# Cosine layer of an attention, experts and cosine kernel: three blocks of token tiles in place of four

## The chip, the cores and the metric

One core of a Trainium2 chip runs the whole kernel in one launch. The metric is the device time of the launch in microseconds (us). TensorE does the matmuls, ScalarE (ACT) and VectorE (DVE) the elementwise work, GpSimd (POOL) some of it and the gathers, SyncE (SP) issues most DMAs. Results of TensorE go to eight banks of 128 x 512 float32.

## The reference

Attention with pooled queries gives x with 1152 rows of 512. A layer of eight experts with the top two per row (`w1`, ReLU, `w2`) gives a new x. Then the cosine layer, which the change is about:

```python
def _moe2_ref(x, w_in, w_out) -> np.ndarray:   # x 1152 x 512, w_in 512 x 2048, w_out 2048 x 512
    h = x @ w_in
    g = h * np.cos(h)
    return (g @ w_out).astype(np.float32)
```

## The kernel before

The 1152 rows are nine tiles of 128. Every float32 operand is kept as a high and a low part, and each product is made of three matmuls (`mm3`, L1043: high x high, high x low, low x high; the matmul itself is L1048).

**The cosine layer** (from L1143, loop at L1454) takes the tiles in blocks, `BLK`: (0, 1), (2, 3), (4, 5) and (6, 7, 8). For each block it runs over f = 0 to 15, the sixteen groups of 128 hidden columns; a step is one (block, f), and the loop runs through the 64 steps in one go.

- `g_mm(b, f)` (L1346): h of all rows of the block in one result bank, twelve matmuls (four groups of inputs x three), each 128 columns wide per tile of the block.
- `g_head` (L1387), `g_cos` (L1403), `g_split` (L1412): cosine by range reduction and the two parts of g = h cos h. The nine instructions go ScalarE L1398 (or L1377), VectorE L1399 to L1401 (or L1378 to L1380), ScalarE Abs and Sin (L1408, L1409 or L1383, L1384), VectorE product (L1410 or L1385), ScalarE `gh` (L1416), VectorE `gl` (L1417). In a block of 256 columns the intermediate r lies in the second half of the same bank, so `gl`, the last instruction, still reads it; in wider blocks it lies in `cr`, and the product is the bank's last reader.
- `o_mm(b, f)` (L1420): for each tile of the block three matmuls of 512 columns, added up over f in one bank per tile (`OA`).

In one turn of the loop, the order is: combine (below), `g_mm` of step i, `o_mm` of step i - 3 (`LAG`, L1453), `g_cos` of step i - 1, `g_head` of step i, `g_split` of step i - 1, then, in the first block only, the split of one more unit of cosine weights into its parts (`conv`, L622: ScalarE L624, then POOL or, at step 6, VectorE L625). Each engine works through its instructions in this order.

**Combining the next block.** While block b runs, the tiles of block b + 1 are made from the outputs of the experts: `comb_load` (L1148, at f in `CL`, and f = 9 for a third tile) gathers two rows per token with two DMAs issued by POOL; `comb` (L1155, at f in `CM`) scales the first on ScalarE into a result bank `CS` (L1166) and adds the second on VectorE (L1167); `comb_tr` (L1180, at f in `CT`) transposes with four short TensorE instructions (L1173) into a `t` bank and copies out with ScalarE (L1185) and VectorE (L1186).

**Result banks.** Of the eight, two have the name `t` (`tb2`, L1001), and at L1335 three are given to `h` (`h_bank`, L1004) and so three to `acc` (`a_bank`, L1007, for `OA`, `CS` and the last expert's third piece). Tiles of one name take its banks in turn, and a new tile waits until the last reader of the old one in that bank is done. `g_mm` of overall step s takes `t` if s mod 3 is 2, else `h`; `comb_t` and `small_weights` (L518) take `t` too.

**The end of a block.** `o_out` (L1443) copies each `OA` with ScalarE to a buffer `os` (three of them) and stores it from SP; the last block goes through `o_last` (L1429), which shares the copies between ScalarE and VectorE, halves the last one and stores from ScalarE's queue. The weights were loaded through a ring of three buffers `raw` (`raw_load`, L607), not used after the first block.

Of the kernel before, what the change touches and what calls it, by code (L numbers as in the profile page):

```python
# [9 lines left out]
F32 = mybir.dt.float32  # L10
F32R = mybir.dt.float32r
# [3 lines left out]
AF = mybir.ActivationFunctionType  # L15
OP = mybir.AluOpType
AX = mybir.AxisListType
PSUM = bass.MemoryType.PSUM
# [4 lines left out]
def attn_moe_cos_kernel(ctx, tc, q, k, v, w_gate, w_noise, noise, w1, w2, w_in, w_out, out):  # L23
    nc = tc.nc
# [3 lines left out]
    DM = H * D  # L28
# [489 lines left out]
    def small_weights(k):  # L518
        m = CNT8[:, 1:2]
        if k:  # L520
            p = tb2()
            nc.tensor.matmul(p[:, 0:2], ONES, FLB, start=True, stop=True)
            nc.vector.tensor_scalar(m, p[:, 0:1], TOP, TOP, op0=OP.mult, op1=OP.min)
            nc.vector.tensor_tensor(CNT, CNT8[:, 0:1], m, op=OP.max)
            return
        nc.vector.tensor_reduce(m, FL, axis=AX.X, op=OP.max)
        nc.vector.tensor_scalar(FLB, m.to_broadcast([128, 2]), 0.0, None, op0=OP.is_gt)
# [68 lines left out]
    NU, NA, RB, NX = 12, 3, 3, 4  # L596
    U, UX, RAW, rawp = [], [], {}, []
# [51 lines left out]
    def advance_c(c):  # L649
        advance(min(c + RB, len(SEQ)), c)  # L650
# [106 lines left out]
    t = t0 = Q2[0, 0] = qk.tile([128, 1216], F32R, name="q2", bufs=3)  # L757
# [16 lines left out]
    c = slice(0, SQ)  # L774
# [30 lines left out]
    c = slice(SQ, 1216)  # L805
# [39 lines left out]
    for n in range(NTOT - 1):  # L845
        hp, hl, t = tiles[n]
# [57 lines left out]
    n = NTOT - 1  # L904
# [92 lines left out]
    mes = ExitStack()  # L997
    mpe = ExitStack()
    mp = [mpe.enter_context(tc.tile_pool(name="moeps", bufs=1, space=PSUM, reuse_waits="tile")), 2]
# [21 lines left out]
    me = mx.enter_context(tc.tile_pool(name="moee", bufs=1, reuse_waits="tile"))  # L1021
# [84 lines left out]

    def y_out(e, st):
        o = ACC.pop((e, st))
        t = mb.tile([128, DM], F32, name="os", bufs=3) if st == 2 else me.tile([128, DM], F32, name="ys", bufs=3)
        n = SW[e][st][1]  # L1110
        if st == 1:
            nc.vector.tensor_copy(t[128 - n:128], o[128 - n:128])
        else:
            nc.scalar.activation(t[128 - n:128], o[128 - n:128], AF.Copy)
        y_store(nc.scalar, e, st, n, t[128 - n:128])
# [24 lines left out]

    DEC, DW = {}, {}

    BLK = [(0, 1), (2, 3), (4, 5), (6, 7, 8)]  # L1143
    G2, CB, CS, X2, LM, hb, hes = {}, {}, {}, {}, {}, [], ExitStack()
    WS = const.tile([128, 2], F32, name="WS")
    RF = const.tile([128, 2, 2, 2], F32, name="RF")
# [1 line left out]
    def comb_load(t):  # L1148
        for j in range(2):
            g = G2[t, j] = hb[0].tile([128, DM], F32, name="g", bufs=4)  # L1150
            nc.gpsimd.indirect_dma_start(
                out=g, out_offset=None, in_=y_d[0:min(t + 1, 3) * 1024],
                in_offset=bass.IndirectOffsetOnAxis(ap=ROWC[:, t, j:j + 1], axis=0))

    def comb(b, i):  # L1155
        t = BLK[b][i]
        g0, g1 = G2.pop((t, 0)), G2.pop((t, 1))
# [16 lines left out]
        return p.rearrange("p (a s) -> p a s", a=4), slice(128 * i, 128 * i + 128)  # L1174

    def x2_tile(b):
        pool, w = (mb, 384) if b % 2 else (hb[0], 256)
        X2[b] = tuple(pool.tile([128, 4, w], F32R, name=f"x2{k}") for k in range(2))

    def comb_tr(b, i):  # L1180
# [55 lines left out]
        nc.scalar.activation(LM["x"][:, :, cs], pv, AF.Copy)  # L1236

    def x2_parts():
        xp_, (xh, xl) = LM["x"], X2[0]
        for h in range(2):  # L1240
            p = tb2()
            ks = slice(2 * h, 2 * h + 2)
            for k in range(2):
                seq = [(y[:, st, 256 * h + 128 * k:256 * h + 128 * k + 128], LM["o"][:, st])
                       for y in LM["y"] for st in range(2)]
                for i, (l, r) in enumerate(seq):
                    nc.tensor.matmul(p[:, 256 * k:256 * k + 256], l, r, start=(i == 0), stop=(i == 3))
            x = xp_[:, ks]
            nc.vector.tensor_tensor(x, p.rearrange("p (a s) -> p a s", a=2), x, op=OP.add)
            nc.scalar.activation(xh[:, ks], x, AF.Copy)  # L1250
            nc.vector.tensor_tensor(xl[:, ks], x, xh.bitcast(F32)[:, ks], op=OP.subtract)

    LA = 6
    YS = (4, 7, 1)
    CL = (2, 6)
    CM = (6, 9, 11)
    CT = (8, 12, 13)
    CO = 4
    LOD = (6,)
    LMS = (18, 25, 26, 27, 28, 34)  # L1260
    NF2 = FF2 // 128
# [14 lines left out]
    for e in range(E_N):  # L1276
        last = e == E_N - 1
        for f in range(8):
            s = 8 * e + f
# [52 lines left out]
    for st in range(2):  # L1332
        y_out(E_N - 1, st)
    mpe.close()
    mp[:] = [mes.enter_context(tc.tile_pool(name="mm2ps", bufs=1, space=PSUM, reuse_waits="tile")), 3]  # L1335
    HS = {(0, 0): h_bank()}
    for f in range(YS[0]):
        y_mm(E_N - 1, f, 2)
# [6 lines left out]
        y_mm(E_N - 1, f, 2)  # L1345
    def g_mm(b, f):  # L1346
        nb = len(BLK[b]) * 128
        p = HS.pop((b, f)) if (b, f) in HS else (tb2 if (NF2 * b + f) % 3 == 2 else h_bank)()
        o = p[:, 0:nb]
        w = unit(NCONV + f)[:, :, 0:512].rearrange("p s (a f) -> p s a f", a=4)  # L1350
        xh, xl = X2[b]
        mm3(o, [(w[:, 0, kd], w[:, 1, kd], xh[:, kd, 0:nb], xl[:, kd, 0:nb]) for kd in range(4)], True, True)
        HS[b, f] = p
# [10 lines left out]
    mb = m2.enter_context(tc.tile_pool(name="m2", bufs=1, reuse_waits="tile"))  # L1364
# [9 lines left out]
    GT, OA = {}, {}  # L1374
# [12 lines left out]
    def g_head(b, f):  # L1387
        nb = len(BLK[b]) * 128
        p = HS[b, f]
        o = p[:, 0:nb]  # L1390
        n, c = (mb.tile([128, 384], F32, name=nm, bufs=2)[:, 0:nb] for nm in ("cn", "cr"))
        if 2 * nb > 512:
            HS[b, f] = (o, c, c)
            cos_arg(n, c, o)
            return
        r = p[:, nb:2 * nb]
        HS[b, f] = (o, r, c)
        nc.scalar.activation(r, o, AF.Identity, scale=1.0 / (2.0 * math.pi), bias=MGC[:, 0:1])  # L1398
        nc.vector.tensor_scalar(n, r, MAGIC, None, op0=OP.subtract)  # L1399
        nc.vector.scalar_tensor_tensor(r, n, -C1, o, op0=OP.mult, op1=OP.add)  # L1400
        nc.vector.scalar_tensor_tensor(r, n, -C2, r, op0=OP.mult, op1=OP.add)  # L1401
# [10 lines left out]
    def g_split(b, f):  # L1412
        nb = len(BLK[b]) * 128
        o, r, c = HS.pop((b, f))
        gh, gl = (mb.tile([128, 384], F32R, name=nm, bufs=4) for nm in ("gh", "gl"))
        nc.scalar.activation(gh[:, 0:nb], r, AF.Copy)  # L1416
        nc.vector.tensor_tensor(gl[:, 0:nb], r, gh.bitcast(F32)[:, 0:nb], op=OP.subtract)  # L1417
        GT[b, f] = (gh, gl)

    def o_mm(b, f):  # L1420
        gh, gl = GT.pop((b, f))
        w = unit(NCONV + f)[:, :, 512:1024]
        for i in range(len(BLK[b])):
            if f == 0:
# [1 line left out]
            c = slice(128 * i, 128 * i + 128)  # L1426
            mm3(OA[b, i], [(gh[:, c], gl[:, c], w[:, 0], w[:, 1])], f == 0, f == NF2 - 1)

    def o_last(b):  # L1429
        n = len(BLK[b])  # L1430
        for i, t in enumerate(BLK[b]):
            s = mb.tile([128, DM], F32, name="os", bufs=3)
            o = OA.pop((b, i))
            if i == n - 1:
                nc.scalar.activation(s[:, 0:256], o[:, 0:256], AF.Copy)
                nc.vector.tensor_copy(s[:, 256:512], o[:, 256:512])
            elif i % 2:
                nc.vector.tensor_copy(s, o)
            else:
                nc.scalar.activation(s, o, AF.Copy)  # L1440
            nc.scalar.dma_start(out[t * 128:(t + 1) * 128], s)

    def o_out(b):  # L1443
        if b == len(BLK) - 1:
            o_last(b)
            return
        for i, t in enumerate(BLK[b]):
            s = mb.tile([128, DM], F32, name="os", bufs=3)
            nc.scalar.activation(s, OA.pop((b, i)), AF.Copy)
            nc.sync.dma_start(out[t * 128:(t + 1) * 128], s)  # L1450

    steps = [(b, f) for b in range(len(BLK)) for f in range(NF2)]
    LAG = 3  # L1453
    for i in range(len(steps) + LAG):  # L1454
        if i < len(steps):
            b, f = steps[i]
            if b + 1 < len(BLK):
                nx = BLK[b + 1]
                for q_, t in enumerate(nx[:2]):
                    if f == CL[q_]:  # L1460
                        comb_load(t)
                if f == 9 and len(nx) > 2:
                    comb_load(nx[2])
                for q_, t in enumerate(nx):
                    if f == CM[q_]:
                        comb(b + 1, q_)
                    if f == CT[q_]:
                        comb_tr(b + 1, q_)
            if i > 1:
                g_mm(b, f)  # L1470
        if i >= LAG:
            b, f = steps[i - LAG]
            o_mm(b, f)
            if f == NF2 - 1:
                o_out(b)
        if 0 < i <= len(steps):
            g_cos(*steps[i - 1])
        if i < len(steps):
            g_head(*steps[i])
        if i == YS[2]:  # L1480
            y_out(E_N - 1, 2)
        if i in (3 * NF2 + 2, 3 * NF2 + 7):
            small_weights(i != 3 * NF2 + 2)
        if 0 < i <= len(steps):
            g_split(*steps[i - 1])
        if i < NF2:
            st_w["lo"] = nc.vector if i in LOD else nc.gpsimd
            advance_c(min(NCONV + i + CO, len(SEQ)))
# [121 lines left out]
```

## Time and profile before

| | |
|---|---|
| time, median of 3 runs (lowest to highest) | 772.87 us (767.8 to 774.36) |
| the profiled execution: its own time, its span | 777.81 us, 776.2 us |
| cosine layer within the span | from about 560 us to 770 us |
| first block, steps g0 to g15 | g0 from 560.2, g15 at 602.7 us |
| last block, steps 48 to 63 | from 698 us |

The profile gives, for one execution, each instruction's start and duration, the idle time of its engine just before it and what released it ("<-DVE gl L1417": VectorE's instruction at line 1417 writing `gl`). "x12" is twelve merged instructions. PE is TensorE. Matmuls overlap at their ends, so the time per matmul is read from the chain of waits, not from the mean of one.

### The profile page before, as it was taken

Reading aid. Unit: us, or ns where it says so; the run is one execution under the profiler, and the core shown is the slowest. Engines: PE = TensorE matmul, PEld = TensorE weight load, DVE = VectorE, ACT = ScalarE, POOL = GpSimd, SP = SyncE. Lnnn points to the kernel's source line nnn. Section 1 sums busy time; section 2 is a strip of 40 time slices with the busy share of each in tenths; the row PEclk is TensorE's granted clock in tenths of the full one; section 3 lists DMA queues with packets and bytes.
Section 4 is the critical chain, followed back from the end, with each engine's and each line's share of the span. In section 5 each row is a group of like instructions: output and inputs, shape, how many; then the busy total and the mean of one; then the engine's idle time right before and its main releaser. Section 6 shows DMA issues by size and latency. Waiting matters only on the chain.

```text
span 776.2 us, 14241 instructions
## 1 busy us (share of the span) xinstructions
PE 742.8 (96%) x4977; PEld 690.5 (89%) x4977; DVE 573.4 (74%) x1235; ACT 529.6 (68%) x1256; POOL 287.1 (37%) x338
## 2 busy tenths in 40 slices
PE   7899999999999987799999999999999999999996
PEld 4699999999999987699899999998889999999895
DVE  5778788778888885368888886776668687785663
ACT  5898799879979842248667766756478665765542
POOL 5978867867868758200000000002067010000000
PEclk9999999999999999799999999999999999999998
DMA  9847757676488716678989989877444110100001
GB/s 219 176 112 186 173 135 170 148 192 147 107 208 295 230 31 235 220 227 298 343 300 328 339 294 324 295 267 244 160 112 141 55 55 2 55 0 28 2 1 43
DMA packets 80125, 133.86 MB, mean 172 GB/s; under 512 B 12394, under 2 KB 42474, under 8 KB 80046
## 3 DMA queue, kind: packets, MB, share of 16 engines
q1 hardware_dynamic: 73230, 110.67, 49.1%
q0 software_dynamic: 5376, 18.40, 6.5%
q10 hardware_dynamic: 1440, 3.80, 1.8%
q8 instruction: 41, 0.67, 0.4%
q14 instruction: 38, 0.31, 0.1%
HBM read 80.99 MB, written 30.29 MB: 143 GB/s over the span
## 4 chain that ended last, share of the span: by engine, by line
PE 82%; DMA 5%; ACT 4%; DVE 3%; issue 3%; POOL 1%; SPq 1%; ACTq 0%; DVEq 0%; POOLq 0%
PE h L1048 22%; PE acc L1048 13%; PE acc L1080 12%; PE s L297 10%; PE pa L369 8%; PE pt L331 8%; PE t L1048 4%; PE t L1040 1%; DMA qd<-ql 1%; DMA raw<-w_d 1%; DMA kb<-sh 1%; PE pt L674 1%; PE t L1097 1%; DMA kt<-st 1%; ACT u L624 1%
## 5 line engine op out<-in xcount | busy, mean ns | idle before, releaser
L316 ACT ACTIVATE p<-s,nm 128x384 f32<-128x384 f32 x216 | 126.1, 593 | 1.2 <-DVE nm L309 0.8
L307 DVE TENSOR_REDUCE nm<-s 128x1 f32<-128x384 f32 x216 | 108.4, 549 | 25.1 <-PE s L297 24.4
L1048 PE MATMUL h<-xe,u 128*128 128x320 f32 (+5 forms) x768 | 122.4, 309 | 2.0 <-issue 2.0
L1048 PEld LDWEIGHTS h<-xe,u 128*128 128x128 f32 x768 | 110.8, 190 | 5.5 <-issue 3.7
L625 DVE TENSOR_TENSOR u<-raw,u 128x1024 fp32r<-128x1024 f32 x66 | 80.5, 1223 | 32.4 <-ACT u L624 32.3
L331 PE MATMUL pt<-ident,p 128*128 128x128 f32 x645 | 93.5, 272 | 0.5 <-ACT st L179 0.3
L297 PE MATMUL s<-kt,q 128*128 128x384 f32 x240 | 84.7, 368 | 4.6 <-DMA kt<-st 2.2
L369 PE MATMUL pa<-eh,v 128*128 128x320 f32 (+1 forms) x279 | 86.5, 324 | 0.0
L344 ACT ACTIVATE eh<-pt 128x384 fp32r<-128x384 f32 x144 | 63.0, 491 | 31.5 <-PE pt L331 29.4
L1135 POOL DMA_DIRECT2D w_d<-dw x16 | 8.5, 534 | 202.7 <-DVE dw L1134 202.7
L369 PE MATMUL pa<-el,v 128*128 128x320 f32 (+1 forms) x279 | 82.3, 309 | 0.0
L624 ACT ACTIVATE u<-raw 128x1024 fp32r<-128x1024 f32 x73 | 76.7, 1055 | 7.0 <-DMA raw<-w_d 3.0
L331 PEld LDWEIGHTS pt<-ident,p 128*128 128x128 f32 x645 | 77.6, 140 | 3.8 <-ACT st L179 0.6
L1080 PE MATMUL acc<-hh,u 128*128 128x320 f32 (+5 forms) x448 | 73.2, 306 | 3.9 <-issue 3.9
L348 DVE TENSOR_TENSOR el<-pt,eh 128x384 fp32r<-128x384 f32 x144 | 73.1, 549 | 4.0 <-ACT eh L344 2.1
L355 POOL TENSOR_TENSOR el<-rw,eh 128x384 fp32r<-128x384 f32 x71 | 71.6, 1009 | 5.9
L1080 PEld LDWEIGHTS acc<-hh,u 128*128 128x128 f32 x448 | 66.1, 192 | 4.1 <-issue 4.1
L1048 PE MATMUL acc<-u,gh 128*128 128x512 f32 x216 | 67.5, 394 | 0.0
L297 PE MATMUL s<-kt,l 128*128 128x384 f32 x198 | 66.4, 338 | 0.0
L1059 ACT ACTIVATE hh<-h 128x320 fp32r<-128x320 f32 (+5 forms) x64 | 26.8, 419 | 44.0 <-PE h L1048 26.2
L1048 PE MATMUL h<-x,u 128*128 128x256 f32 (+1 forms) x384 | 56.8, 297 | 0.0
L1048 PEld LDWEIGHTS h<-x,u 128*128 128x128 f32 x384 | 54.3, 190 | 2.2
(272 smaller groups left out, 1648.7 us busy)
## 6 DMA issues: line engine op xcount, KB each, us to landing
raw<-in_moe_w_dram SPq DMA_DIRECT2D x64, 512.0 KB, 4.9
raw<-in_moe_w_in_dram SPq DMA_DIRECT2D x16, 512.0 KB, 6.0
raw<-in_moe_w_out_dram SPq DMA_DIRECT2D x16, 512.0 KB, 5.8
w_d<-dw POOLq DMA_DIRECT2D x16, 512.0 KB
raw<-w_d SPq DMA_DIRECT2D x14, 512.0 KB, 4.8
xg_d<-ZERO SPq DMA_DIRECT2D x10, 512.0 KB, 7.5
vn<-in_v_dram SPq DMA_DIRECT2D x16, 288.0 KB, 3.4
q<-sh SPq DMA_DIRECT2D x14, 304.0 KB, 5.6
```

The source lines that it names most:

```text
L297: nc.tensor.matmul(o, l, r, start=(m == 0), stop=(m == len(mm) - 1))
L307: nc.vector.tensor_reduce(NM[n][:, i:i + 1], SB[n][i][:, 0:384], axis=AX.X, op=OP.max, negate=True)
L316: nc.scalar.activation(P[n][i], SB[n][i][:, 0:384], AF.Exp, bias=NM[n][:, 3:4], accum_out=SUMS[:, t, 2 * hp + hl, i:i + 1])
L331: nc.tensor.transpose(p[:, c], P[n][j][:, c], ident)
L344: nc.scalar.activation(t_dst(n, j)[0], t_src(n, j), AF.Copy)
L348: nc.vector.tensor_tensor(el, t_src(n, j), ef, op=OP.subtract)
L355: nc.gpsimd.tensor_tensor(el, rw, ef, op=OP.subtract)
L369: nc.tensor.matmul(st["p"][:, 0:w], V2[hp, hl, b][:, VC[c] if hp + b else c, :], (EH, EL)[s][:, c, EB[g]:EB[g] + w], start=(c == 0 and s = ...
L624: nc.scalar.activation(b[:, 0], r, AF.Copy)
L625: st_w["lo"].tensor_tensor(b[:, 1], r, b.bitcast(F32)[:, 0], op=OP.subtract)
L1048: nc.tensor.matmul(o, l, r, start=first and i == 0, stop=last and i == len(seq) - 1)
L1080: nc.tensor.matmul(ACC[e, d][:, 0:CAPS[e]], w[:, i, 128 * d:128 * d + 128], r[:, 0:CAPS[e]], start=f == 0 and r is hh and i == 0, stop=f = ...
```

## The change

`BLK` becomes (0, 1), (2, 3, 4) and (5, 6, 7, 8): 48 steps, the last block with matmuls of 512 columns. `h` has two banks and `acc` four; odd steps of `g_mm` take a `t` bank, even ones an `h` bank. The third and fourth tile of the next block are loaded, combined and transposed at times of their own (`CL`, `CM`, `CT`). The widths of `cn`, `cr`, `gh` and `gl` become 512 with one, two, three and three buffers (before: 384 with two, two, four, four); the block inputs of even blocks get 512 columns. `o_last` goes: all blocks copy with ScalarE into buffers of the `raw` ring and store from SP.

```diff
@@ -1106,7 +1106,7 @@
 
     def y_out(e, st):
         o = ACC.pop((e, st))
-        t = mb.tile([128, DM], F32, name="os", bufs=3) if st == 2 else me.tile([128, DM], F32, name="ys", bufs=3)
+        t = mb.tile([128, DM], F32, name="os", bufs=1) if st == 2 else me.tile([128, DM], F32, name="ys", bufs=3)
         n = SW[e][st][1]
         if st == 1:
             nc.vector.tensor_copy(t[128 - n:128], o[128 - n:128])
@@ -1140,7 +1140,8 @@
 
     DEC, DW = {}, {}
 
-    BLK = [(0, 1), (2, 3), (4, 5), (6, 7, 8)]
+    BLK = [(0, 1), (2, 3, 4), (5, 6, 7, 8)]
+    BW = 512
     G2, CB, CS, X2, LM, hb, hes = {}, {}, {}, {}, {}, [], ExitStack()
     WS = const.tile([128, 2], F32, name="WS")
     RF = const.tile([128, 2, 2, 2], F32, name="RF")
@@ -1174,7 +1175,7 @@
         return p.rearrange("p (a s) -> p a s", a=4), slice(128 * i, 128 * i + 128)
 
     def x2_tile(b):
-        pool, w = (mb, 384) if b % 2 else (hb[0], 256)
+        pool, w = (mb, 384) if b % 2 else (hb[0], BW)
         X2[b] = tuple(pool.tile([128, 4, w], F32R, name=f"x2{k}") for k in range(2))
 
     def comb_tr(b, i):
@@ -1236,7 +1237,7 @@
         nc.scalar.activation(LM["x"][:, :, cs], pv, AF.Copy)
 
     def x2_parts():
-        xp_, (xh, xl) = LM["x"], X2[0]
+        xp_, (xh, xl) = LM["x"], (t[:, :, 0:256] for t in X2[0])
         for h in range(2):
             p = tb2()
             ks = slice(2 * h, 2 * h + 2)
@@ -1252,9 +1253,9 @@
 
     LA = 6
     YS = (4, 7, 1)
-    CL = (2, 6)
-    CM = (6, 9, 11)
-    CT = (8, 12, 13)
+    CL = (2, 6, 9, 12)
+    CM = (6, 9, 11, 14)
+    CT = (8, 12, 13, 15)
     CO = 4
     LOD = (6,)
     LMS = (18, 25, 26, 27, 28, 34)
@@ -1332,7 +1333,7 @@
     for st in range(2):
         y_out(E_N - 1, st)
     mpe.close()
-    mp[:] = [mes.enter_context(tc.tile_pool(name="mm2ps", bufs=1, space=PSUM, reuse_waits="tile")), 3]
+    mp[:] = [mes.enter_context(tc.tile_pool(name="mm2ps", bufs=1, space=PSUM, reuse_waits="tile")), 2]
     HS = {(0, 0): h_bank()}
     for f in range(YS[0]):
         y_mm(E_N - 1, f, 2)
@@ -1345,7 +1346,7 @@
         y_mm(E_N - 1, f, 2)
     def g_mm(b, f):
         nb = len(BLK[b]) * 128
-        p = HS.pop((b, f)) if (b, f) in HS else (tb2 if (NF2 * b + f) % 3 == 2 else h_bank)()
+        p = HS.pop((b, f)) if (b, f) in HS else (tb2 if (NF2 * b + f) % 2 else h_bank)()
         o = p[:, 0:nb]
         w = unit(NCONV + f)[:, :, 0:512].rearrange("p s (a f) -> p s a f", a=4)
         xh, xl = X2[b]
@@ -1388,7 +1389,7 @@
         nb = len(BLK[b]) * 128
         p = HS[b, f]
         o = p[:, 0:nb]
-        n, c = (mb.tile([128, 384], F32, name=nm, bufs=2)[:, 0:nb] for nm in ("cn", "cr"))
+        n, c = (mb.tile([128, BW], F32, name=nm, bufs=k)[:, 0:nb] for nm, k in (("cn", 1), ("cr", 2)))
         if 2 * nb > 512:
             HS[b, f] = (o, c, c)
             cos_arg(n, c, o)
@@ -1412,7 +1413,7 @@
     def g_split(b, f):
         nb = len(BLK[b]) * 128
         o, r, c = HS.pop((b, f))
-        gh, gl = (mb.tile([128, 384], F32R, name=nm, bufs=4) for nm in ("gh", "gl"))
+        gh, gl = (mb.tile([128, BW], F32R, name=nm, bufs=3) for nm in ("gh", "gl"))
         nc.scalar.activation(gh[:, 0:nb], r, AF.Copy)
         nc.vector.tensor_tensor(gl[:, 0:nb], r, gh.bitcast(F32)[:, 0:nb], op=OP.subtract)
         GT[b, f] = (gh, gl)
@@ -1426,26 +1427,9 @@
             c = slice(128 * i, 128 * i + 128)
             mm3(OA[b, i], [(gh[:, c], gl[:, c], w[:, 0], w[:, 1])], f == 0, f == NF2 - 1)
 
-    def o_last(b):
-        n = len(BLK[b])
+    def o_out(b):
         for i, t in enumerate(BLK[b]):
-            s = mb.tile([128, DM], F32, name="os", bufs=3)
-            o = OA.pop((b, i))
-            if i == n - 1:
-                nc.scalar.activation(s[:, 0:256], o[:, 0:256], AF.Copy)
-                nc.vector.tensor_copy(s[:, 256:512], o[:, 256:512])
-            elif i % 2:
-                nc.vector.tensor_copy(s, o)
-            else:
-                nc.scalar.activation(s, o, AF.Copy)
-            nc.scalar.dma_start(out[t * 128:(t + 1) * 128], s)
-
-    def o_out(b):
-        if b == len(BLK) - 1:
-            o_last(b)
-            return
-        for i, t in enumerate(BLK[b]):
-            s = mb.tile([128, DM], F32, name="os", bufs=3)
+            s = rawp[0].tile([128, 1024], F32, name="raw", bufs=RB)[:, 0:DM]
             nc.scalar.activation(s, OA.pop((b, i)), AF.Copy)
             nc.sync.dma_start(out[t * 128:(t + 1) * 128], s)
 
@@ -1456,11 +1440,9 @@
             b, f = steps[i]
             if b + 1 < len(BLK):
                 nx = BLK[b + 1]
-                for q_, t in enumerate(nx[:2]):
+                for q_, t in enumerate(nx):
                     if f == CL[q_]:
                         comb_load(t)
-                if f == 9 and len(nx) > 2:
-                    comb_load(nx[2])
                 for q_, t in enumerate(nx):
                     if f == CM[q_]:
                         comb(b + 1, q_)
@@ -1479,8 +1461,8 @@
             g_head(*steps[i])
         if i == YS[2]:
             y_out(E_N - 1, 2)
-        if i in (3 * NF2 + 2, 3 * NF2 + 7):
-            small_weights(i != 3 * NF2 + 2)
+        if i in (len(steps) - 14, len(steps) - 9):
+            small_weights(i != len(steps) - 14)
         if 0 < i <= len(steps):
             g_split(*steps[i - 1])
         if i < NF2:
```

## Rows read from the trace of the kernel before

**Rows 1.** The profile's busy time: us, share of the span, instructions.

```profile
PE 742.8 (96%) x4977; PEld 690.5 (89%) x4977; DVE 573.4 (74%) x1235; ACT 529.6 (68%) x1256; POOL 287.1 (37%) x338
```

**Rows 2.** Windows: length, busy us (instructions) of PE, PEld, DVE, ACT, POOL, clock, DMA.

```profile
580.00:590.00 10.00, 8.45 (x55) 7.44 (x55) 8.43 (x19) 9.03 (x19) 7.86 (x5) 1.00 0.73 234
590.00:600.00 10.00, 10.00 (x65) 8.96 (x65) 8.32 (x22) 7.75 (x18) 7.85 (x6) 1.00 0.17 54
...
740.00:750.00 10.00, 10.00 (x51) 8.91 (x50) 5.86 (x12) 5.27 (x10) 0.00 (x0) 1.00 0.01 2
```

**Rows 3.** The chain that ended last: start us, us, what; later blocks.

```profile
607.12 1.39 PE acc L1048 x6
...
712.73 2.10 PE h L1048 x12
714.83 2.08 PE acc L1048 x9
```

**Rows 4.** The same chain, first block: g9, and the transposes at step 12.

```profile
585.50 1.43 PE h L1048 x12
...
593.97 0.44 PE t L1173 x4
```

**Rows 5.** Timeline of TensorE, first block: transposes at step 8, then g8.

```profile
580.32 0.66 PE L1173 MATMUL t<-ident,cm 128*128 128x128 f32 x4
582.42 1.69 PE L1048 MATMUL t<-x,u 128*128 128x256 f32 x12 [1.45 <-DVE gl L1417]
```

**Rows 6.** Timeline of VectorE, first block: splits of g5, g7, g11; a combine.

```profile
581.95 0.42 DVE L1417 TENSOR_TENSOR gl<-t,gh 128x256 fp32r<-128x256 f32 x1
...
588.14 0.42 DVE L1417 TENSOR_TENSOR gl<-h,gh 128x256 fp32r<-128x256 f32 x1
589.39 0.75 DVE L1167 SCALAR_TENSOR_TENSOR cm<-g,WT,acc 128x512 f32<-128x512 f32 x1 [0.84 <-DMA g<-y_d,ROWC]
...
599.68 0.42 DVE L1417 TENSOR_TENSOR gl<-t,gh 128x256 fp32r<-128x256 f32 x1
```

**Rows 7.** Timeline of ScalarE, first block: the first instruction on g11.

```profile
595.28 0.43 ACT L1398 ACTIVATE t<-t,MGC 128x256 f32<-128x256 f32 x1
```

**Rows 8.** Groups by line, 600 us to the end: busy us, mean ns of one, idle before.

```profile
L1167 DVE SCALAR_TENSOR_TENSOR cm<-g,WT,acc 128x512 f32<-128x512 f32 x5 | 3.7, 739 | 0.0
...
L1166 ACT ACTIVATE acc<-g,WT 128x512 f32<-128x512 f32 x5 | 3.4, 687 | 0.0
```

**Rows 9.** Timeline of POOL: gathers and one weight split.

```profile
582.78 1.55 POOL L1151 DMA_INDIRECT g<-y_d,ROWC  x1 [0.31 <-issue]
...
588.42 2.40 POOL L625 TENSOR_TENSOR u<-raw,u 128x1024 fp32r<-128x1024 f32 x1 [0.73 <-ACT u L624]
...
626.61 0.95 POOL L1151 DMA_INDIRECT g<-y_d,ROWC  x1 [0.30 <-DVE cm L1167]
```

**Rows 10.** A window behind a gather, columns as in rows 2.

```profile
630.00:632.00 2.00, 2.00 (x13) 1.74 (x13) 1.90 (x5) 1.57 (x4) 0.00 (x0) 1.00 0.00 0
```

**Rows 11.** Timeline after the last `g_mm`: first and last instruction of its chain.

```profile
761.06 0.58 ACT L1377 ACTIVATE cn<-h,MGC 128x384 f32<-128x384 f32 x1 [0.82 <-PE h L1048]
...
765.60 0.56 DVE L1417 TENSOR_TENSOR gl<-cr,gh 128x384 fp32r<-128x384 f32 x1 [0.59 <-ACT gh L1416]
```

**Rows 12.** Timeline of the end: first copy, last matmul, last store.

```profile
767.90 0.60 ACT L1440 ACTIVATE os<-acc 128x512 f32<-128x512 f32 x1 [2.33 <-PE acc L1048]
...
768.83 0.39 PE L1048 MATMUL acc<-u,gl 128*128 128x512 f32 x1
...
770.62 0.34 ACTq L1441 DMA_DIRECT2D out_dram<-os  x1
```

**Rows 13.** DMA issues: KB each, median us to landing.

```profile
out_dram<-os SPq DMA_DIRECT2D x6, 256.0 KB, 2.0
```

**Rows 14.** A window at the end, columns as in rows 2.

```profile
771.00:773.00 2.00, 0.00 (x0) 0.00 (x0) 0.00 (x0) 0.00 (x0) 0.00 (x0) 0.74 0.42 142
```

**Rows 15.** A window near the start, columns as in rows 2.

```profile
14.00:18.00 4.00, 3.74 (x22) 3.56 (x20) 1.55 (x4) 3.95 (x15) 1.86 (x1) 0.57 1.06 243
```

## The prediction

> **What bounds the kernel now.** I read the busy shares first: TensorE is busy for 96% of the span, far ahead of every other engine [rows 1]. A share is a mean over stages, so next come the ten-microsecond windows of the stage that the change touches. From 590 us on TensorE works 10.00 us in every 10.00 while VectorE and ScalarE have a quarter to a half of their time free; only the window 580 to 590 has 8.45 us, and there ScalarE is at 9.03 [rows 2]. So the stage is bound by TensorE, except at one place in the first block, where the weights of the cosine layer are still being split and ScalarE is full. The chain of waits gives what one step costs TensorE: 1.43 us for the twelve matmuls of `g_mm` at 256 columns and 1.39 us for the six of `o_mm` over two tiles; in the three-tile block 2.10 and 2.08 us [rows 3, 4]. Whatever delays TensorE after 585 us delays the end by as much, since it has no free time left to catch up in.
>
> I write g7 for `g_mm` of step 7 of the first block, o7 for its `o_mm`, C8 for the transposes of a combined tile at step 8. TensorE runs C, g(i), o(i-3) in each step.
>
> **The change part by part.**
>
> *Fewer, wider matmuls.* Per step f the four blocks cost 3 x 1.43 + 2.10 = 6.39 us of `g_mm`. After, there are 256, 384 and 512 columns. The trace has no `g_mm` of 512 columns; nine `o_mm` matmuls of 512 columns take 2.08 us, so twelve take 2.77; scaling 2.10 by 512/384 gives 2.80, the other bound [rows 3, 4]. I take 2.77, measured at this very width: 1.43 + 2.10 + 2.77 = 6.30 us. Over 16 steps that saves 1.4 us (1.0 by the other bound). The 27 matmuls of `o_mm` per step and the seven transposed tiles stay. So nearly all columns are still streamed; only 192 starts go, at 1.4/192 = 7 ns each. The Trainium skill ("TensorE: Matmul & The Clock Gate", section "Wait — 56ns, not 53.3ns?") puts the fixed part of a matmul at about 2.5 ns; by it the saving would be an estimated 0.5 us and the sum 0.9 us worse. The rows decide.
>
> *Four banks for `g_mm` in place of five, and what waits for them.* In the first block ScalarE runs several steps behind TensorE, so a bank is released late. g5's bank is released by the last instruction of its split, at 581.95 + 0.42 = 582.37, and g8, which takes that bank next, stood idle for 1.45 us and began at 582.42 [rows 5, 6]. g7's split ends at 588.14 + 0.42 = 588.56 [rows 6]. Before, g7 had one of three `h` banks, and the next to take it came late enough. After, odd steps take the two `t` banks in turn, and each C takes a turn too: g5 has one, g7 the other, C8 the first, g9 the second, that of g7. So C8 waits for the split of g5 (from 580.32 [rows 5] to 582.42; g8, now on an `h` bank that is free, follows at 582.86, and the old stall of 1.45 us is spent here), and then g9 waits for the split of g7 until 588.60. Before, it began at 585.50 [rows 4]. ScalarE and VectorE don't come earlier for this: their work up to there is the same, and they lag behind TensorE. That is 3.1 us on the path. From both sides: 0 if the bank is not the one waited for, 3.1 if it is; the row of g8 shows exactly this kind of wait, so I take 3.1. Even steps have two `h` banks, four steps apart, as the nearest pairs of before had: no cost.
>
> *A third tile combined inside the first block.* The block that follows now has three tiles, so C13 is new there (one fewer later: no TensorE time). From 588.60 in steps of 2.82: g11 at 594.24, ending 595.67; then o8, C12 (0.44 [rows 4]), g12, o9 up to 600.32. C13 takes g11's bank. Before, g11's ScalarE chain began at 595.28 and its split ended at 599.68 + 0.42 = 600.10 [rows 6, 7]. After, it starts behind the third tile's scaling, 0.69 us more on ScalarE, at about 596.0, and VectorE has 0.74 us more (the same two instructions of other tiles [rows 8]): the release comes near 601.3, a stall of 1.0 us. The new gathers sit on POOL behind the split that ends at 588.42 + 2.40 = 590.82, so they issue at 591.0 and 592.3. A gather issued at 626.61 had its bytes moved before 630 [rows 9, 10], some 3.4 us at most, so the second is there by 595.7, about when ScalarE has scaled the first: VectorE hardly waits. Behind them on POOL are only the last two weight splits, 2.5 us later, wanted from 600 on. Bounds: 0 if the release comes by 600.3; 4.4 if the gather takes as long as the one of 582.78, which VectorE awaited until 589.39 [rows 6, 9]: 6.6 us, so 3.4 later. The DMA engines were at 0.73 then and are at 0.17 after 590 [rows 2]; I take 1.0.
>
> *The later blocks.* There ScalarE keeps up: after the last `g_mm` of 384 columns its chain starts at 761.06 and the whole split ends at 765.60 + 0.56 = 766.16, 5.1 us after [rows 11]; the bank is free before that. With a C between, a bank comes back after o, C, g, o: 2.08 + 0.44 + 2.10 + 2.08 = 6.7 us. A combined tile puts up to 0.74 us twice on each engine in between [rows 8], so 6.6 us at worst: just covered; if it is not, the rival below prices it. The rings of three `gh`/`gl` cost nothing: the slot written is read by the `o_mm` right behind the own `g_mm`, gone 2.08 us after it, and the writes are the last two instructions, 0.6 us each, of a chain of 5.1 us. One `cn` costs nothing: ScalarE's next writer already stands behind an instruction that waits for its last reader. A fourth result accumulates in a fourth bank, free by then.
>
> *The end.* After the last `g_mm` three `o_mm` of 2.77 us follow, 8.3 us; the chain of 5.1 us at 384 columns is at most 6.8 at 512: covered. Then the copies. Before, ScalarE, VectorE and both halves shared them and the last store was issued at 770.62, 1.40 us after the last matmul's end (768.83 + 0.39) [rows 12]. After, four copies of 0.60 us run on ScalarE alone, each result 0.69 us after the one before, into a ring of three `raw` buffers. The fourth shares the first's buffer and must await its store. With T the first result's end: copied at T + 0.64, stored from SP at T + 0.66, landed 2.0 us later (the stores of the earlier blocks [rows 13]) at T + 2.66; copy 4 ends at T + 3.3, its store is issued at T + 3.33, and T + 2.04 is TensorE's end: 1.29 us behind it, against 1.40. The sum is -0.1 us. Ends: -0.7 without that wait (the copy would start with the result), +2.0 if the store's landing takes twice as long; I take the measured 2.0.
>
> **Sum.** -1.4 + 3.1 + 1.0 - 0.1 = +2.6 us. Made against the profiled execution: 777.8 (776.2 of span and 1.6 around it) becomes 780.4. That execution stands 4.9 us above the median of the runs shown, so the forecast is 772.9 + 2.6 = **775.5 us**, 0.3% slower. A measurement of this kernel tells about 1%, 7.7 us, from no change: this lies inside.
>
> **The rivals.** *No wait for the banks.* If the `t` banks come free in time (another order of the turns), 3.1 and 1.0 go: -1.5 us, 771.4. For it: the last use of a bank is known only for the order of before. Against: g8's 1.45 us. Chance 0.16.
>
> *The clock falls at the stall.* TensorE would idle from 580.3 to 582.4 and again from 585.7 to 588.6, 2.9 us. At the end of the trace the granted clock has a mean of 0.74 from 771 to 773, so between 1.00 and 0.50 it fell near 772, some 2.7 us after the last matmul ended at 769.22 [rows 12, 14]. From 14 to 18 us its mean was 0.57 with TensorE busy 3.74 of 4.00 us [rows 15]: nearly all at the lower level, 1.2 GHz, which loses some 1.7 us of work. Then the time is 775.5 + 1.7 = 777.2. For: the length of the stall. Against: ScalarE's lag takes up part of any loss before C13. Chance 0.20. The same page of the Trainium skill (section "What's actually happening") says that the gate closes when the engine idles and that activity opens it; the rows agree.
>
> *Slower by over 1%: the wait returns in the second block.* If ScalarE still lagged there as in the first, where g7 (ended by 578.8) gave its bank back at 588.56, 9.8 us later, every bank due after 6.7 us would stall TensorE for 3.1 us: at g9, C13 and g15 of that block, 9.3 us together, so 775.5 + 9.3 = 784.8. It decides as soon as the release comes more than 6.7 us after the `g_mm`. For: one more tile is combined there than before. Against: ScalarE's 6 us or less per ten in the later windows [rows 2] and the 5.1 us [rows 11]. Chance 0.12.
>
> **How the numbers follow.** The forecast (0 to 4.4 for C13, the tail's ends) has 0.48 and lies at 773 to 778. The range reaches from the no-wait case less the tail's gain and some scatter (the three runs shown differ by 6.6 us) to the clock case with a late gather: 769.5 to 781.0; it leaves out the returning wait and tails. Faster by over 1% needs 7.7 us, for which nothing here pays; the remaining 0.04 is for what I don't see. Slower by over 1%: the 0.12 of the last rival. Same: 0.48 + 0.16 + 0.20 = 0.84.
>
> **What would show it.** Right: C8 idle until about 582.4 with VectorE's `gl` as releaser, g9 idle nearly 3 us on the `gl` of g7, about 1 us before C13, none in the two later blocks; twelve `g_mm` matmuls of 512 columns in 2.77 us; the fourth copy starting when SP's first store lands. Wrong: TensorE busy without a gap after 580, a g9 released by something else, or gaps at steps 9 to 15 of the second block.

## The result, and the profile after

The changed kernel takes 776.55 us (median of seven runs, 775.0 to 777.4) against 770.78 us for the kernel before, run beside it: a ratio of 1.0070, 95% interval 1.0047 to 1.0094, or 3.6 to 7.2 us slower. It lies within the forecast range of 769.5 to 781.0 us and, as forecast, within 1% of before. But the loss, 5.8 us between the medians, is about twice the 2.6 us forecast, and the profile shows that the terms behind it were not the right ones.

Where TensorE waits, in the cosine layer and just ahead of it (timeline of TensorE, changed kernel):

```profile
541.22 1.92 PE L1048 MATMUL h<-xe,u 128*128 128x320 f32 x12
...
546.11 0.63 PE L1174 MATMUL t<-ident,g 128*128 128x128 f32 x4
549.38 1.21 PE L1048 MATMUL acc<-u,hh 128*128 128x512 f32 x2 [2.65 <-DVE ys L1112]
...
580.34 0.66 PE L1174 MATMUL t<-ident,cm 128*128 128x128 f32 x4 [2.03 <-DVE gl L1418]
580.75 1.68 PE L1048 MATMUL h<-x,u 128*128 128x256 f32 x12
584.39 1.70 PE L1048 MATMUL t<-x,u 128*128 128x256 f32 x12 [0.56 <-DVE x L1187]
...
597.06 0.66 PE L1174 MATMUL t<-ident,cm 128*128 128x128 f32 x4 [0.68 <-DVE x L1187]
599.13 1.69 PE L1048 MATMUL t<-x,u 128*128 128x256 f32 x12 [1.42 <-DVE gl L1418]
```

The wait at 549.38 ends with VectorE's copy of the last expert's second piece (timeline of the changed kernel):

```profile
548.65 0.68 DVE L1112 COPY ys<-acc 128x512 f32<-128x512 f32 x1
```

The same place of the kernel before, which had no wait ahead of the third piece of the last expert; there the third piece starts 2.17 us before that copy does:

```profile
547.28 1.92 PE L1048 MATMUL h<-xe,u 128*128 128x320 f32 x12
...
552.58 0.63 PE L1173 MATMUL t<-ident,g 128*128 128x128 f32 x4
...
552.96 0.70 PE L1048 MATMUL acc<-u,hh 128*128 128x512 f32 x2
...
555.13 0.69 DVE L1112 COPY ys<-acc 128x512 f32<-128x512 f32 x1
```

Lines after L1143 have moved by one, so L1418 is `gl` and L1187 the VectorE copy of the transposed tile. C8 (580.34), g9 (584.39), C13 (597.06) and g13 (599.13) wait, 4.69 us in all, where before g8 alone waited 1.45 [rows 5]. A wait of 2.65 us at 549.38 is new, and behind it two matmuls take 1.21 us instead of 0.70. The windows there tell why (columns as in rows 2):

```profile
545.00:549.00 4.00, 1.66 (x8) 0.93 (x8) 3.79 (x7) 2.46 (x4) 0.00 (x0) 1.00 0.50 153
549.00:553.00 4.00, 3.62 (x9) 2.89 (x10) 0.33 (x1) 0.00 (x0) 0.00 (x0) 0.57 0.29 110
553.00:557.00 4.00, 4.00 (x29) 3.64 (x28) 0.80 (x2) 1.23 (x2) 0.00 (x0) 1.00 0.02 4
```

The granted clock fell to a mean of 0.57, that is to the lower of its two levels for most of these 4 us. From 600 us to the last matmul TensorE never waits. There the steps are cheaper than forecast (chain that ended last, second and third block):

```profile
620.37 2.08 PE acc L1048 x9
622.45 2.10 PE h L1048 x12
...
674.37 2.72 PE h L1048 x12
677.09 2.04 PE acc L1048 x9
...
726.87 2.72 PE h L1048 x12
729.59 2.72 PE acc L1048 x12
```

At the end, the fourth copy waits for the first store, as forecast (timeline; "x3" and "x4" are merged):

```profile
765.66 1.96 ACT L1433 ACTIVATE raw<-acc 128x512 f32<-128x512 f32 x3 [3.37 <-PE acc L1048]
766.29 3.10 SPq L1434 DMA_DIRECT2D out_dram<-raw  x4
768.44 0.60 ACT L1433 ACTIVATE raw<-acc 128x512 f32<-128x512 f32 x1 [0.82 <-DMA out_dram<-raw]
```

One trap lies in the spans. The profiled executions are 776.2 us before and 774.9 after, the wrong way round: in the one of before something else took 6 us more, ahead of the code that changed (the last expert's last twelve matmuls of `h<-xe` start at 547.28 there and at 541.22 after). So I count from that instruction, called the anchor below, in stretches that end at the start of g1, the start of g15, the end of the last matmul and the end of the span. All are differences of times in the traces:

| us | to g1 | g1 to g15 | g15 to last matmul | to the end | sum |
|---|---|---|---|---|---|
| before | 15.71 | 39.71 | 166.52 | 6.98 | 228.92 |
| changed | 19.80 | 43.84 | 162.81 | 7.23 | 233.68 |
| difference | +4.09 | +4.13 | -3.71 | +0.25 | +4.76 |

The sum agrees with the timed 3.6 to 7.2 us.

### The profile page after: what moved, and what is told of

It is laid out like the page before. It is cut to its first block, busy times and chain, and to the rows that moved or that the text cites. A ratio compares the mean times of both kernels' runs of the same rounds, so it can differ in the third digit from the quotient of the medians.

```text
span 774.9 us, 13756 instructions
## 1 busy us (share of the span) xinstructions
PE 742.7 (96%) x4785; PEld 682.2 (88%) x4785; DVE 560.1 (72%) x1153; ACT 520.7 (67%) x1193; POOL 290.9 (38%) x338
## 4 chain that ended last, share of the span: by engine, by line
PE 79%; ACT 5%; DVE 5%; DMA 4%; POOL 3%; issue 2%; SPq 1%; POOLq 0%; DVEq 0%; ACTq 0%
PE h L1048 18%; PE acc L1048 13%; PE s L297 10%; PE acc L1080 10%; PE pa L369 9%; PE pt L331 8%; PE t L1048 6%; PE pt L674 2%; PE t L1040 2%; POOL xg_d L589 1%; ACT u L624 1%; DMA xg_d<-X,ROW 1%; PE t L1097 1%; DMA kt<-st 1%; PE pt L178 1%
## 5 line engine op out<-in xcount | busy, mean ns | idle before, releaser
L297 PEld LDWEIGHTS s<-kt,q 128*128 128x128 f32 x240 | 44.7, 190 | 12.7 <-ACT p L316 7.5
L354 POOL TENSOR_SCALAR eh<-rw 128x384 fp32r<-128x384 f32 x71 | 36.5, 515 | 45.0 <-ACT rw L352 42.7
L369 PEld LDWEIGHTS pa<-el,v 128*128 128x128 f32 x279 | 52.9, 190 | 0.0
```

What stands on the lines that cost most here:

```text
L297: nc.tensor.matmul(o, l, r, start=(m == 0), stop=(m == len(mm) - 1))
L369: nc.tensor.matmul(st["p"][:, 0:w], V2[hp, hl, b][:, VC[c] if hp + b else c, :], (EH, EL)[s][:, c, EB[g]:EB[g] + w], start=(c == 0 and s = ...
```

## The experiments

My theory after the result: all of the loss is waits for result banks (a wrong bank at the opening of the set, and the transposes' turns in the first block), which hide a gain of over 3 us from wider matmuls. Rivals: the waits come from ScalarE and VectorE being full, so that other banks would only move them; or the blocks themselves cost.

**The opening of the banks.** `e1_free_bank` changes only the order in which the names of the set are first used:

```diff
+    PRE.append(tb2())
     HS = {(0, 0): h_bank()}
```
```diff
-        p = tb2()
+        p = PRE.pop() if PRE else tb2()
```

(the second in `comb_t`; `PRE` is a list that starts empty, and the bank taken early goes to the next call of `comb_t`).

> The changed kernel, with the new set of result banks opened in the order t, h, acc instead of h, acc, t, so that the last expert's third piece begins in a bank that nobody uses any more. Theory (bank): the idle 2.65 us before that piece is the wait for the copy of the last expert's second piece out of the same bank; the lower clock behind it is its consequence. Expected: no idle time there over 0.5 us, clock 1.00 throughout, 4 us less than the changed kernel, about 772.5 us. Rival (late copies): TensorE would have to wait for ScalarE and VectorE there anyway; expected 776 to 777 us and the idle time at the next wait.

Measured: 1.0012 of before, run beside it (95% interval 0.9996 to 1.0029), 0.6% less than the changed kernel. All ratios below are to before in the same way. The third piece follows the transposes at once (timeline of TensorE):

```profile
549.32 0.63 PE L1176 MATMUL t<-ident,g 128*128 128x128 f32 x4
549.71 0.70 PE L1048 MATMUL acc<-u,hh 128*128 128x512 f32 x2
```

The stretch to g1 is 15.47 us (15.71 before). So the new wait was for the bank. The late copies of the rival are still in the program: VectorE's copy of the second piece starts at 551.85, 2.1 us after the third piece has begun, and TensorE does not wait for it. The waits of the first block stayed, and in this execution the clock, expected at 1.00 throughout, fell behind them (windows):

```profile
597.00:601.00 4.00, 3.06 (x15) 2.87 (x16) 2.23 (x6) 1.85 (x5) 1.95 (x3) 0.74 0.73 203
601.00:604.00 3.00, 3.00 (x17) 2.67 (x17) 1.69 (x5) 0.89 (x2) 0.00 (x0) 0.78 0.16 59
```

so that g1 to g15 took 45.52 us, 1.7 more than in the changed kernel's execution.

**The turns of the t banks.** `e2_comb_in_acc`:

```diff
-        p = tb2()
+        p = (a_bank if b == 1 else tb2)()
```

> The changed kernel, with the transposes of the three tiles combined in the first block in an accumulator bank that is free there, so that they take no turn of the t banks. Theory (bank): the 4.7 us of idle TensorE at steps 8 to 13 (2.03, 0.56, 0.68 and 1.42) go, expected about 772 us. Rival (full ScalarE): ScalarE is the bound of the first block, so that freed banks only move the wait to the matmuls that need the split g; expected over 775 us, with the idle time at the matmuls of the second product.

Measured: 1.0005 (0.9991 to 1.0020), 0.65% or 5 us less than the changed kernel, as the bank theory has it. g1 to g15 takes 39.99 us, 3.85 less. The wait at the opening stayed (2.64 us), and behind it the clock stayed at 1.00 here (window):

```profile
554.00:558.00 4.00, 3.30 (x17) 2.75 (x18) 0.65 (x2) 0.00 (x0) 0.00 (x0) 1.00 0.35 131
```

The rival has a small part: waits of 0.16 to 0.43 us take their place, the longest for the split g,

```profile
594.35 0.50 PE L1048 MATMUL acc<-u,gl 128*128 128x512 f32 x1 [0.43 <-DVE gl L1418]
```

and with the added transposes 39.99 us is no better than the 39.71 of before, which still held 1.45 us of waiting.

**Both.** `e3_both` has both edits.

> Both edits together. If both are bank waits and add up: 776.6 - 4.1 - 4.7 = about 768 us, 3 us below the kernel before, a ratio of 0.996 to it. If ScalarE's pace bounds the first block: 771 to 773 us.

Measured: 768.68 us, 0.9938 of before (0.9912 to 0.9964), faster than both kernels; the two gains add up. From the anchor on it takes 14.89 + 39.70 + 162.80 + 6.82 = 224.21 us, 4.7 below before. What is left in the first block is no longer a bank (timeline of TensorE):

```profile
586.39 0.50 PE L1048 MATMUL acc<-u,gl 128*128 128x512 f32 x1 [0.16 <-DVE gl L1421]
...
591.24 0.66 PE L1176 MATMUL acc<-ident,cm 128*128 128x128 f32 x4 [0.41 <-DVE cm L1170]
```

**The banks without the blocks.** `e5_banks_only` is the kernel before with

```diff
-space=PSUM, reuse_waits="tile")), 3]
+space=PSUM, reuse_waits="tile")), 2]
...
-(tb2 if (NF2 * b + f) % 3 == 2 else h_bank)()
+(tb2 if (NF2 * b + f) % 2 else h_bank)()
```

> The kernel before, four blocks, with only the banks of the change: two for h, four for acc, every odd step in a t bank. Theory (bank): the idle time at the opening of the banks (4.1 us with its clock) and 1 to 2 us more at steps 8 to 13 come without any change of blocks; expected 775 to 777 us. Rival (blocks): the third tile combined in the first block is what costs; expected 771 us, as before.

Measured: 1.0106 (1.0057 to 1.0155; 779.29 us, four runs of 778.13 to 785.77). That is above the 775 to 777 us expected. With four blocks and no third tile in the first, the waits at the opening, at C8 and at g9 are there; g13, the last line, does not wait (timeline of TensorE, then a window):

```profile
550.26 0.73 PE L1048 MATMUL acc<-u,hh 128*128 128x512 f32 x2 [2.66 <-DVE ys L1112]
...
579.63 0.66 PE L1173 MATMUL t<-ident,cm 128*128 128x128 f32 x4 [2.12 <-DVE gl L1417]
...
583.68 1.69 PE L1048 MATMUL t<-x,u 128*128 128x256 f32 x12 [0.57 <-DVE x L1186]
...
595.50 1.61 PE L1048 MATMUL t<-x,u 128*128 128x256 f32 x12
```

```profile
550.00:554.00 4.00, 3.73 (x20) 3.19 (x21) 0.21 (x1) 0.24 (x1) 0.00 (x0) 1.00 0.26 95
```

From the anchor on: 18.09 + 40.86 + 168.11 + 7.23 = 234.29 us, 5.4 over before. So the split of the banks alone makes the kernel as slow as the whole change does, or slower. Here the clock stayed at 1.00 behind the 2.66 us. The rival is right in one part: g1 to g15 takes 40.86 us here and 43.84 in the changed kernel, so 3.0 us of that stretch, the waits at C13 and g13 and the 0.44 of C13 itself, come only where the third tile is combined in the first block as well. And 1.6 us are lost after g15, where TensorE waits for `gl` three times, 0.77 us in all; the rest was not traced.

**The blocks without the waits.** `e6_four_blocks` is the kernel before, with its end, the banks of the change and both remedies (the edits of e1 and e5, and `a_bank if b else tb2` in `comb_t`).

> The kernel before with its four blocks and its own end, but with two banks for h and four for acc, the order t, h, acc, and the transposes of combined tiles in accumulator banks: all bank waits gone, blocks as before. It parts the blocks from the banks. Theory (three blocks pay by themselves): wider matmuls save 3.3 us, so this is 3.3 us slower than the kernel of both edits, ratio 0.998 to before, and TensorE shows no idle time over 0.5 us in the cosine layer. Rival (the waits were all): as fast as the kernel of both edits, 0.994.

Measured: 770.77 us, 0.9994 (0.9978 to 1.0011). Parted from e3_both by 0.56%, and from e4_tail, timed beside it, by 0.32%, 2.5 us. In the traces the difference to e3_both is mainly in the last long stretch, 166.51 against 162.80 us (the two stretches before it differ by +1.07 and -0.67). That holds the transposes of one tile more (0.44), so 3.3 us are the blocks'. The waits were not all. Cleared of waits, four blocks gain nothing measurable on the kernel before: its 1.45 us are partly given back to the split of g, as in e2 (timeline of TensorE):

```profile
586.36 0.50 PE L1048 MATMUL acc<-u,gl 128*128 128x512 f32 x1 [0.43 <-DVE gl L1420]
```

**What a start costs.** `e7_split_g` is e3_both with

```diff
+        cut = 256 if nb == 512 else nb
+        for c0 in range(0, nb, cut):
+            cs = slice(c0, c0 + cut)
...
```

around the `mm3` of `g_mm`, on the columns `cs`.

> The kernel of both edits, with each matmul of 512 columns of the first product in the last block issued as two of 256: 192 more matmuls, the same columns, banks and waits. Theory (starts cost, and narrow matmuls slow the wide ones beside them): a step of the last block goes from 2.72 + 2.72 us to 2.86 + 2.77, 0.19 us more, 3.0 us in all, ratio 0.998 to before. Rival (only the starts cost): 2.86 + 2.72, 2.2 us in all. Rival (7 ns per start was a reading error): no change, 0.994.

Measured: 0.9986 (0.9965 to 1.0007). A step of the last block in e7 (chain that ended last),

```profile
703.39 2.87 PE t L1048 x24
706.26 2.75 PE acc L1048 x12
```

and in e3_both:

```profile
702.92 2.72 PE t L1048 x12
705.64 2.72 PE acc L1048 x12
```

It is 0.18 us more a step, 2.9 us over 16, close to the theory's 0.19: 0.15 us for twelve more starts, 12 ns each (with a weight load of its own: the profiles count 4785 matmuls and as many loads in e3_both, 4977 of both in e7), and 0.03 of the 0.05 expected for twelve `o_mm` matmuls, which run slower beside narrow ones though nothing in them changed. g15 to the last matmul is 165.68 us against 162.80.

**The end.** `e4_tail` is e3_both with

```diff
+            if i == 3:
+                s = mb.tile([128, DM], F32, name="os", bufs=1)
...
+            if b == len(BLK) - 1 and i % 2:
+                nc.vector.tensor_copy(s, OA.pop((b, i)))
```

> The kernel of both edits, with the end changed: of the last block's four results the second and fourth are copied by VectorE, the fourth into a buffer of its own, so that it no longer awaits the first one's store. Theory (the ring of three costs at the end): the last store is issued about 0.75 us after the last matmul instead of 1.4, expected 0.6 us less than the kernel of both edits, too little for the times, to be read in the profile. Rival (the end is set by what follows the last store): the store comes earlier, but the span after the last matmul stays at 6.8 to 7.2 us.

Measured: 768.57 us, 0.9962 (0.9946 to 0.9979); by time it cannot be told from e3_both. The last store is issued early (timeline),

```profile
755.94 0.69 DVE L1440 COPY os<-acc 128x512 f32<-128x512 f32 x1 [0.61 <-PE acc L1048]
756.66 0.33 SPq L1443 DMA_DIRECT2D out_dram<-os  x1
```

0.76 us after the last matmul's end at 755.90, but the span ends 7.60 us after it (6.82 in e3_both). The rival holds in that an earlier last store did not bring an earlier end, though 7.60 us is above the 6.8 to 7.2 that it named. These are single executions: among the kernels whose end is that of the change, the stretch is 6.77 us in e1 and 7.23 in the changed kernel. What sets the end behind the store was not tried.

## Why the prediction was right or wrong

- *TensorE bounds the stage, and a delay passes to the end:* right. After 600 us it never waits, and the stretches sum to the result.
- *Fewer, wider matmuls, -1.4 us:* right in sign, undersized; it was -3.3 us (3.71 less the 0.44 of the transposes moved). The step that failed is taking 2.77 us for twelve matmuls of 512 columns from `o_mm` beside narrow ones, and leaving `o_mm` itself as it was. In a block that has only wide ones the twelve take 2.72, and the matmuls of `o_mm` drop from 231 to 227 ns as well (2.08/9 and 2.72/12). Per step of f, `g_mm` goes from 6.39 to 6.25 us and `o_mm` from 6.25 to 6.19, 0.20 us less, 3.2 over 16 steps. The 7 ns per start were 12 by e7. The Trainium skill ("TensorE: Matmul & The Clock Gate", section "Wait — 56ns, not 53.3ns?") gives 2.5 ns, which would leave an estimated 0.5 us; for these matmuls, each with its own weight load, the measurement decides against it.
- *g9 waits for the split of g7, +3.1 us:* wrong. "Each C takes a turn too: g5 has one, g7 the other, C8 the first, g9 the second" failed. C8 took g5's bank and waited, as said (2.03 us); but g9 waited for C8's bank, with `x L1187` as its releaser, for 0.56 us; a g9 released by something else was a sign of being wrong that the prediction named. The releasers of all four waits fit banks given not in strict turn, as the kernel was described, but to the next tile the bank whose last reader stands first in the program: C8's copies stand at the head of step 8, g7's split at its end. The "no wait" rival had named another order of the turns; it was right in that much, but waits came at C13 and g13 instead.
- *C13, +1.0 us:* wrong in its place. The release of g11's bank was the wait, but it fell on g13 (1.42 us), and C13 waited 0.68 us for C12's copies. The two steps together were forecast at 4.1 and gave 3.7 (4.13 less the 0.44 of C13 itself): the sum held by luck, through a compensation. Two readings were off as well: the upper bound of this term should be 4.2 (1.0 + 6.6 - 3.4), not 4.4, and VectorE, said to have at least a quarter of its time free from 590 us on, had 17% from 590 to 600 (8.32 of 10.00 us busy).
- *Nothing at the opening of the set:* the largest error, +4.1 us that no step of the prediction had. I followed the banks within the new set and not which banks of the closed one they lie on. With three for `h` the third piece's bank was not that of the second piece, since it starts 2.17 us before the second piece is copied; with two it is, by the releaser `ys L1112`, and VectorE does that copy late. In e1 another order of first use takes the wait away. About 2.65 us are the wait; the other 1.6 are the clock in this execution (e5, at a clock of 1.00, is only 2.38 over before there).
- *The later blocks:* right, no wait, and no sign of the rival in which the wait returns.
- *The end, -0.1 us:* the steps were right (last copy behind the first store, issue 1.4 us after the last matmul, as before), but in e4 the end does not follow that store, so no run shows the term; the measured +0.25 is within the scatter of single executions.
- *The clock:* a rival at 0.20, for g9. It fell, but behind the unforeseen wait, where the clock's mean was 0.57 and it cost about 1.6 us (the third piece's first twelve matmuls take 4.46 us from 549.38 to the next transposes at 553.84, and 2.85 before). "The rows agree" went too far: rows 14 show a fall behind idle time, but rows 15 only a low mean. A rise is seen here: the mean is 0.57 from 549 to 553, with TensorE busy 3.62 of 4.00 us, and 1.00 from 553 on.

By terms: -3.3 + 3.7 + 4.1 + 0.25 = 4.8, against -1.4 + 3.1 + 1.0 - 0.1 = 2.6. That the time fell within the range is partly luck: the unforeseen 4.1 met 1.9 more gain than forecast. And 775.5 came within 1.1 us of 776.55 because the three runs that it starts from have a median of 772.87 us; the seven beside the changed kernel have 770.78, from which the forecast would have been 773.4.

## What to carry to other kernels

When the number of buffers under a name changes, list the physical bank of every tile on both sides of each pool's opening, by the order in which last readers stand in the program: the costliest wait here was between two pools, and an edit that only changes the order of first use removed it. When a resource split and a tiling change come together, time each without the other; here the tiling was worth 3.3 us, and the waits that came with the split, with the clock behind one of them, cost nearly 8 (4.1 and 3.7), about 2.5 of them only together with the third tile. Count a trace from an instruction that both kernels share, not from its start.

## What the runs showed of the hardware

The clock after a short wait is not a fixed price. A wait of about 2.65 us at the same place was followed by 4 us at a mean of 0.57 in the changed kernel and by 1.00 in e5 (2.66 us) and in e2 (2.64 us); behind 1.42 us and the waits ahead of it, the clock fell in e1 (0.74, then 0.78) and not in the changed kernel (1.00). And the pace of a float32 matmul of 512 columns depends on its neighbours: 2.08 us for nine (231 ns) beside 384 columns, 2.04 for nine and 2.72 for twelve (both 227 ns) beside 512, and 2.75 (229 ns) beside 256 in e7, at a clock of 1.00. Why was not settled.
